# Windowed attention and a gated feed-forward block on one core: score bursts of three head pairs and paired value bursts at fixed places, half 1 reordered, batch 1's products on VectorE

## The chip, the cores and the metric

The kernel runs on one core of a Trainium2 chip. The metric is the device time of one execution in microseconds (us). Every kernel was run beside runs of the kernel before on the same chip. Profiles are of one execution each; their span, from the first to the last instruction, is some 1.8 us less than the device time. The record's verdicts call a difference under 2% the same; where I call a smaller one a gain or a loss, its 95% interval lies on one side of 1.

## The reference

Four batches of 8 heads, 768 tokens, head size 64. A query sees 8 global keys and the last 96 keys, with a bias that grows with distance. The attention output, as 3072 tokens of 512, goes through a gated feed-forward block.

```python
def _attn_ref(q, k, v, n_global, n_local):            # (4, 8, 768, 64) each; 8, 96
    scores = scale * np.matmul(q, k.transpose(0, 1, 3, 2))
    rel = pos[:, None] - pos[None, :]
    keep = (pos[None, :] < n_global) | ((rel >= 0) & (rel < n_local))
    scores = np.where(keep, scores - slope * dist, -1e9)
    a = np.exp(scores - scores.max(-1, keepdims=True))
    return np.matmul(a / (a.sum(-1, keepdims=True) + 1e-9), v)

def _moe_ref(x, w_gate, w_val, w_out):                # 512 -> 1536 -> 512
    g = x @ w_gate
    return (g / (1 + np.exp(-g))) * (x @ w_val) @ w_out
```

## The kernel before

The feed-forward block runs in 8 tiles of 384 tokens; a batch is two tiles ("halves"). A tile has 12 rounds: a gate product, a value product and, interleaved, a quarter of an output product of an earlier tile. A round with all three takes 1.95 us. Of the eight PSUM banks, four (a0 to a3, the "a-banks") go round among the bursts, three among gate and value products, and one holds an output product. The attention of the next half is slipped in between as bursts: transposes of q and k (tile 1 alone; later batches are turned by DMA transposes, "turns" below), scores of a head pair (row-tiled, 64*128), and denominators and numerators of a quad of heads (column-tiled, 128*32).

```python
def scores(self, bk, mul_eng, put_off):        # one head pair, one bank of keys
    sc = banks("sc")                           # two of the a-banks of PSUM
    ...                                        # matmuls, two heads side by side
    if put_off: later.append(exps)             # ScalarE: two exps into `at`
    else:       exps()
    later.append(mask)                         # at *= mask, on VectorE or GpSimd

def values(self, half, bank, mul_eng):         # one quad of heads
    den = bank("den"); self.weigh(half, den, None)
    for side in range(2):
        num = bank("num"); self.weigh(half, num, side)
        nc.scalar.copy(out=src, in_=num[:, 0:TB])
    later.append(lambda: self.invert(den))     # VectorE: transpose, reciprocal
    later.append(spread)                       # VectorE: 1/den; then x = num * 1/den
    ...                                        # on VectorE for batch 0, else on GpSimd

def fetch(b, *hps):                            # turn by DMA, issued from SyncE
    if hps[0] == 0: turn_ends(b)               # kE: the last 48 keys of all pairs
    for hp in hps:  pairs[b, hp].transposes_dma()    # kT, qT of pair hp

def first(b):                                  # tile 1
    return [[tr(b, 0), tr(b, 1)], [sc(b, 0, 0), sc(b, 0, 1)], [tr(b, 2), tr(b, 3)],
            [sc(b, 1, 0), sc(b, 1, 1)], [sc(b, 2, 0), sc(b, 2, 1)], [va(b, 0, 0)],
            [sc(b, 3, 0), sc(b, 3, 1)], [], [va(b, 1, 0)]]
# steps are dealt out evenly among the products; `later` is worked off one item per product
```

Loads go out from GpSimd's queue in program order, so a load can stand behind a product that GpSimd has to make. The fourth early output product stands in round 1 of tile 1.

The softmax here doesn't subtract the row's maximum and nothing guards it: scores larger than these inputs give would overflow.

Of the kernel before, what the change touches and what calls it, by code (L numbers as in the profile page):

```python
# [9 lines left out]
FP32 = mybir.dt.float32  # L10
# [27 lines left out]
def kernel(  # L38
# [117 lines left out]
    def stage_rows(b):  # L156
        qst[b] = sb2.tile([128, NP, J, 2, D], FP16, name="qst", tag="qst")
        kst[b] = sb2.tile([128, NP, J, 2, D], FP16, name="kst", tag="kst")
        kend[b] = sb2.tile([128, H, D], FP16, name="kend", tag="kend", bufs=1)
        nc.gpsimd.memset(kend[b], 0.0)  # L160
        nc.sync.dma_start(out=kend[b][0:NG], in_=kG[:, b])
        for hp in range(NP):
            pair = kG[:, b, 2 * hp:2 * hp + 2, :].rearrange("p h d -> p (h d)")
            nc.sync.dma_start(
                out=kst[b][0:NG, hp].rearrange("p t e d -> p t (e d)"),
                in_=pair.unsqueeze(1).broadcast_to([NG, J, 2 * D]))
# [9 lines left out]
    kG = sb.tile([NG, B, H, D], FP16, name="kG")  # L176

    def load_globals():
        for dst, src in ((kG, k), (vG, v)):
            nc.gpsimd.dma_start(  # L180
                out=dst[:, 1:].rearrange("p b h d -> p (b h) d"),
                in_=src[1:, :, 0:NG, :].rearrange("b h p d -> p (b h) d"))
# [55 lines left out]
    def banks(name, dt=FP32):  # L238
        return [bank(name, dt) for _ in range(2)]

# [15 lines left out]
    class Pair:  # L256
# [97 lines left out]
        def scores(self, bk, mul_eng, put_off):  # L354
            hp = self.hp
            sc = banks("sc")
# [45 lines left out]
    class Quad:  # L402
# [33 lines left out]
        def invert(self, den):  # L436
            dT = sb2.tile([128, TB], FP32, name="dT", tag="dT")
            self.dR = sb2.tile([128, TB // 32], FP32, name="dR", tag="dR")
            nc.vector.transpose(dT, den[:, 0:TB])  # L439
            nc.vector.reciprocal(  # L440
                out=self.dR, in_=dT.rearrange("p (n i) -> p n i", i=32)[:, :, 0])
# [10 lines left out]
        def values(self, half, bank, mul_eng):  # L452
# [3 lines left out]
            for side in range(2):  # L456
                num = bank("num")
                self.weigh(half, num, side)
                src = sb2.tile([128, TB], FP32, name="ns", tag="ns")
                nc.scalar.copy(out=src, in_=num[:, 0:TB])  # L460
                srcs.append(src)
# [25 lines left out]

    hTs = {}
# [3 lines left out]
    def products(t, f, which, c0, c1, dst=None):  # L492
        if f == 0 and which == 0 and c0 == 0:
            hTs[t] = sb2.tile([128, NFF, TB], FP16, name="hT", tag="hT", bufs=3)
        if c0 == 0:
            if dst is None:
                dst = single("gv"[which] + "ps", state["x"][gv.get("n", 0) % len(state["x"])])
                gv["n"] = gv.get("n", 0) + 1
            gv[f, which] = dst
# [141 lines left out]
    def sc(b, hp, bk):  # L641
        on_vector = b < 2 or bk < 2 or hp % 2 == 0
        return lambda: pairs[b, hp].scores(bk, nc.vector if on_vector else nc.gpsimd, bool(later))

    def va(b, g, half):
        return lambda: quads[b, g].values(half, bank, nc.vector if b == 0 else nc.gpsimd)
# [17 lines left out]
    def second(b):  # L664
        return [[sc(b, 0, 2), sc(b, 1, 2)], [sc(b, 2, 2), sc(b, 3, 2)],
                [va(b, 0, 1)], [va(b, 1, 1)]]

# [8 lines left out]
    def first(b):  # L676
        return [[tr(b, 0), tr(b, 1)], [sc(b, 0, 0), sc(b, 0, 1)], [tr(b, 2), tr(b, 3)],
                [sc(b, 1, 0), sc(b, 1, 1)], [sc(b, 2, 0), sc(b, 2, 1)], [va(b, 0, 0)],
                [sc(b, 3, 0), sc(b, 3, 1)], [], [va(b, 1, 0)]]

    def both(b):

        n = b + 1

        return [[sc(b, 0, 2), sc(b, 1, 2)], [sc(b, 2, 2), sc(b, 3, 2), fetch(n, 0, 1)],
                [va(b, 0, 1)], [va(b, 1, 1)],
                [sc(n, 0, 0), sc(n, 0, 1), fetch(n, 2, 3)], [sc(n, 1, 0), sc(n, 1, 1)],
                [va(n, 0, 0)], [sc(n, 2, 0), sc(n, 2, 1)],
                [sc(n, 3, 0), sc(n, 3, 1)], [va(n, 1, 0)]]

    half1 = [[trh(0), trh(1)], [trh(2), trh(3)], [sch(0)], [sch(1)],
             [va(0, 0, 1)], [sch(2)], [sch(3)], [va(0, 1, 1)]]
# [3 lines left out]
    def ff(t, f0, f1, n_out=(0,)):  # L696
# [5 lines left out]
        (ff(1, 0, 12, (0, 1, 1, 1)), first(1), 5.0, 0.2),  # L702
        (ff(2, 0, 12, (1,)) + ff(3, 0, 12, (1,)), both(1), 6.0, 0.4),
        (ff(4, 0, 12, (1,)) + ff(5, 0, 12, (1,)), both(2), 6.0, 0.4),
        (ff(6, 0, 12, (1,)), second(3), 6.0, 0.4),
# [14 lines left out]
    for b, base, rate, v_at in ((2, 19, 2.0, (27, 28, 29, 30, 32, 33, 34)), (3, 43, 1.4, (54, 55, 56, 57, 61, 62, 63))):  # L720
# [12 lines left out]
    outs = [(t, i, part) for t in range(NT - 1) for i in range(3) for part in range(4)]  # L733
    for tiles, steps, tail, owed in stretches:
        groups = []
# [3 lines left out]
        work = sum(g[0] for g in groups)  # L739
        quota = len(steps) / (work - tail)  # L740
        for w, t, f, which in groups:
# [8 lines left out]
            else:  # L750
                gate_or_val(t, f, which, NC if t == 0 and f < 2 else 0)
                for fn in after.pop((t, f, which), []):
                    fn()
            owed += w * quota
            while owed >= 1.0 and steps:
                run_later(len(later))
                for step in steps.pop(0):
                    step()
# [42 lines left out]
```

## Time and profile before

| | before |
|---|---|
| device time, median of 6 runs | 248.66 us (247.84 to 250.19) |
| span of the profile | 247.4 us |
| TensorE busy | 96% |
| VectorE, ScalarE, GpSimd busy | 65%, 53%, 47% |

TensorE streams nearly all the time, so the questions are where it waits and what a burst costs beside its own streaming. The waits of TensorE (who waited for whom: us in total, times, longest) and the granted clock in 40 slices (9 is 90% of full speed or more) of the kernel before:

```profile
PE trs L293 <- DMA q<-in_q_dram: 1.4, 3, 0.6
...
PE gps L502 <- POOL xT L464: 1.1, 2, 0.6
...
PE num L429 <- DMA vS<-in_v_dram: 0.6, 1, 0.6
...
PEclk9999999999999999999999999999999999999999
```

### The profile page before, as it was taken

To read this page: it belongs to the slowest core of one execution; us is meant where nothing else is said; L and a number is where in the kernel's file an instruction comes from. 1 tells how busy PE (TensorE), PEld (TensorE's weight loads), DVE (VectorE), ACT (ScalarE), POOL (GpSimd) and SP (SyncE) were. 2 spreads that over 40 slices of the span, in tenths; PEclk is the share of its full clock that TensorE was granted. 3 is DMA by queue.
4 is the path that set the end of the run, shared out by engine and by line. 5 is a ranking of instruction groups with operands and counts; after the bars stand their busy time and mean duration, and the time that the engine had idled before them with its cause. 6 is when DMAs were issued, how large, how long until landed. Compare 5 with 4: busy or idle time off the path is not lost.

```text
span 247.4 us, 6076 instructions
## 1 busy us (share of the span) xinstructions
PE 238.3 (96%) x2428; PEld 134.8 (54%) x2428; DVE 159.9 (65%) x346; ACT 130.2 (53%) x289; POOL 116.2 (47%) x139
## 2 busy tenths in 40 slices
PE   8898889999998999999999999999999999999994
PEld 5454455555554555555555555555555555555543
DVE  5778656678784767776775576676766666555510
ACT  5736568786753644555734734656635534332321
POOL 8999895344199915407429678603030342200000
PEclk9999999999999999999999999999999999999999
DMA  8999999999279998912919999921001101100122
GB/s 154 164 175 168 186 166 194 202 163 141 69 55 141 137 166 119 146 51 51 85 45 107 82 156 178 176 54 44 30 15 45 42 3 42 43 21 24 42 88 85
DMA packets 86644, 25.10 MB, mean 101 GB/s; under 512 B 72800, under 2 KB 83672, under 8 KB 86616
## 3 DMA queue, kind: packets, MB, share of 16 engines
q0 software_dynamic: 67472, 14.05, 68.0%
q1 hardware_dynamic: 18584, 10.30, 18.1%
q8 instruction: 19, 0.31, 0.6%
q10 hardware_dynamic: 560, 0.36, 0.5%
q14 instruction: 9, 0.07, 0.1%
HBM read 28.67 MB, written 6.29 MB: 141 GB/s over the span
## 4 chain that ended last, share of the span: by engine, by line
PE 74%; DMA 12%; POOL 10%; issue 1%; DVE 0%; ACT 0%; POOLq 0%
PE ops L531 23%; PE vps L502 21%; PE gps L502 21%; DMA qst<-in_q_dram 5%; DMA vS<-in_v_dram 5%; PE sc L365 3%; DMA q<-in_q_dram 3%; PE num L429 3%; PE den L429 2%; POOL vS L170 1%; POOL wv L212 1%; POOL xT L464 1%; POOL k L118 1%; POOL qst L193 1%; PE trs L267 1%
## 5 line engine op out<-in xcount | busy, mean ns | idle before, releaser
L515 DVE SCALAR_TENSOR_TENSOR sl<-th,gps 128x384 f32<-128x384 f32 x94 | 52.0, 553 | 51.9 <-ACT th L513 51.2
L513 ACT ACTIVATE th<-gps 128x384 f32<-128x384 f32 x94 | 46.4, 494 | 65.9 <-PE gps L502 64.2
L502 PE MATMUL gps<-xT,wg 128*128 128x384 f16 x376 | 77.2, 326 | 1.4 <-POOL xT L464 1.1
L502 PE MATMUL vps<-xT,wv 128*128 128x384 f16 x376 | 76.6, 326 | 0.6 <-DVE sl L515 0.6
L531 PE MATMUL ops<-wo,hT 128*128 128x512 f16 x276 | 73.1, 379 | 0.0
L519 DVE TENSOR_TENSOR hT<-vps,sl 128x384 f16<-128x384 f32 x94 | 51.9, 552 | 10.3 <-PE vps L502 3.0
L464 POOL TENSOR_TENSOR xT<-ns,rb 128x384 f16<-128x384 f32 x24 | 23.8, 1014 | 69.2 <-DVE rb L445 69.2
L502 PEld LDWEIGHTS <-wg 128*128 128x128 f16 x384 | 36.3, 98 | 33.4 <-issue 1.7
L502 PEld LDWEIGHTS <-wv 128*128 128x128 f16 x384 | 36.1, 98 | 27.0 <-issue 3.3
L531 PEld LDWEIGHTS <-hT 128*128 128x128 f16 x276 | 26.2, 98 | 23.7 <-issue 0.7
L373 ACT ACTIVATE at<-sc 128x432 f16<-128x432 f32 x72 | 33.2, 536 | 9.6 <-PE sc L365 9.6
L170 POOL DMA_DIRECT2D vS<-in_v_dram x28 | 24.8, 899 | 7.5 <-DMA wo<-in_moe_w_out_dram 3.5
L537 ACT ACTIVATE osb<-ops 128x512 f32<-128x512 f32 x23 | 13.7, 598 | 17.1 <-PE ops L531 17.1
L460 ACT COPY ns<-num 128x384 f32<-128x384 f32 x28 | 12.1, 483 | 9.4 <-PE num L429 8.5
L384 DVE TENSOR_TENSOR at<-at,masks 128x864 f16<-128x864 f16 x20 | 12.1, 607 | 7.0 <-ACT at L373 7.0
L193 POOL DMA_DIRECT2D kst<-in_k_dram x16 | 14.1, 888 | 0.0
L193 POOL DMA_DIRECT2D qst<-in_q_dram x16 | 13.7, 867 | 0.0
L384 POOL TENSOR_TENSOR at<-at,masks 128x864 f16<-128x864 f16 x4 | 7.3, 1821 | 13.3 <-ACT at L373 13.3
L348 ACT ACTIVATE at<-sc 128x432 f16<-128x432 f32 (+2 forms) x32 | 11.6, 447 | 3.0 <-PE sc L340 2.8
L429 PE MATMUL num<-at,vS 128*32 128x216 f16 (+6 forms) x560 | 12.3, 226 | 0.6 <-DMA vS<-in_v_dram 0.6
L429 PEld LDWEIGHTS <-vS 128*32 128x32 f16 x560 | 9.7, 95 | 1.2 <-DMA vS<-in_v_dram 1.0
L439 DVE STREAM_TRANSPOSE dT<-den 128x384 f32<-128x384 f32 x16 | 9.2, 578 | 1.6 <-PE den L429 1.6
(71 smaller groups left out, 175.0 us busy)
## 6 DMA issues: line engine op xcount, KB each, us to landing
out_dram<-osb SPq DMA_DIRECT2D x23, 256.0 KB
vS<-in_v_dram POOLq DMA_DIRECT2D x24, 120.0 KB, 6.2
wg<-in_moe_w_gate_dram POOLq DMA_DIRECT2D x12, 128.0 KB, 5.3
wv<-in_moe_w_val_dram POOLq DMA_DIRECT2D x12, 128.0 KB, 5.3
wo<-in_moe_w_out_dram POOLq DMA_DIRECT2D x4, 384.0 KB, 9.2
qst<-in_q_dram POOLq DMA_DIRECT2D x16, 96.0 KB, 3.6
kst<-in_k_dram POOLq DMA_DIRECT2D x16, 90.0 KB, 3.7
kst<-in_k_dram POOLq DMA_DIRECT2D x2, 384.0 KB, 13.0
```

What stands on the lines that cost most here:

```text
L170: nc.gpsimd.dma_start(out=vSs[b][NG:NG + n, c, :, :], in_=v[b, :, KC * c:KC * c + n, :].rearrange("h p d -> p h d"))
L193: nc.gpsimd.dma_start(out=st[b][p0:p0 + n, h // 2, :, h % 2, :], in_=src[b, h, 0:n * J].rearrange("(t p) d -> p t d", p=n))
L373: nc.scalar.activation(out=at[:, hi, :], in_=sc[hi][:, 0:BANK], func=AF.Exp, scale=scale)
L384: mul_eng.tensor_mul(at, at, m[:, :, o:o + BANK])
L429: nc.tensor.matmul(dst[r, o:o + n], lhsT=ones[:, 0:32] if side is None else vals[:, 4 * g + j, side::2], rhs=pairs[b, 2 * g + j // 2].at[c ...
L464: mul_eng.tensor_mul(self.x_out(half, side), srcs[side], self.rb)
L502: nc.tensor.matmul(gv[f, which][:, 0:TB], lhsT=w[:, c, 128 * f:128 * f + 128], rhs=x_of(t)[:, c, :], start=(c == 0), stop=(c == NC - 1))
L513: nc.scalar.activation(out=th, in_=dst[:, 0:TB], func=AF.Tanh, scale=0.5)
L515: nc.vector.scalar_tensor_tensor(out=sl, in0=th, scalar=1.0, in1=dst[:, 0:TB], op0=AluOp.add, op1=AluOp.mult)
L519: nc.vector.tensor_mul(hTs[t][:, f, :], dst[:, 0:TB], gv["sl"])
L531: nc.tensor.matmul(ops, lhsT=hTs[t][:, f, 128 * i:128 * i + 128], rhs=wo[:, f, :], start=(f == 0), stop=(f == NFF - 1))
L537: nc.scalar.mul(out=osb, in_=ops, mul=0.5)
```

## The change

Its intent is to switch TensorE's tiling less often: three head pairs to a score burst, two quads to a value burst, each at a fixed place behind an output product. Two spare PSUM banks of the gate and value products serve the first pair. Half 1 of batch 0 is reordered. Products of x for batch 1 move from GpSimd to VectorE, those of a paired burst are shared between the two, and the loads of batch 3 are placed earlier. The rest of the diff is room: dT has one buffer in place of two, ns four, and kG goes without batch 0. The core of the diff:

```diff
+    def spare(name):                       # one of the three banks of gate and value
+        tag = state["x"][gv.get("n", 0) % len(state["x"])]
...
+    def both_values(b, half):              # two denominators, inverted at once, then
+        ...                                # four numerators; first quad's x on GpSimd,
+                                           # second quad's on VectorE
     def va(b, g, half):
-        return lambda: quads[b, g].values(half, bank, nc.vector if b == 0 else nc.gpsimd)
+        return lambda: quads[b, g].values(half, bank, nc.vector if b < 2 else nc.gpsimd)
...
-    def first(b):
-        return [[tr(b, 0), tr(b, 1)], [sc(b, 0, 0), sc(b, 0, 1)], [tr(b, 2), tr(b, 3)], ...
+    def first(t, b):                       # (tile, round): behind that round's products
+        return {(t, 1): [tr(b, 0), tr(b, 1)],
+                (t, 3): [sc(b, (0, 0), (0, 1), (1, 0))],
+                (t, 4): [tr(b, 2), tr(b, 3)],
+                (t, 6): [sc(b, (1, 1), (2, 0), (2, 1))],
+                (t, 7): [va(b, 0, 0)],
+                (t, 8): [sc(b, (3, 0), (3, 1))],
+                (t, 9): [va(b, 1, 0)]}
+    def both(t, b):
+        n = b + 1
+        return {(t, 0): [sc(b, (0, 2), (1, 2), (2, 2)), fetch(n, 0, 1)],
+                (t, 4): [sc(b, (3, 2), (0, 0, n), (1, 0, n)), fetch(n, 2, 3)],
+                (t, 8): [vas(b, 1)],
+                (t + 1, 0): [sc(n, (0, 1), (1, 1), (2, 0))],
+                (t + 1, 4): [sc(n, (2, 1), (3, 0), (3, 1))],
+                (t + 1, 8): [vas(n, 0)]}
...
-    half1 = [[trh(0), trh(1)], [trh(2), trh(3)], [sch(0)], [sch(1)],
-             [va(0, 0, 1)], [sch(2)], [sch(3)], [va(0, 1, 1)]]
+    half1 = [[trh(0), trh(1)], [sch(0)], [trh(2), trh(3)], [sch(1)],
+             [sch(2)], [va(0, 0, 1)], [sch(3)], [va(0, 1, 1)]]
...                                         # batch 3's loads of q, k (base) and v (list)
-    (3, 43, 1.4, (54, 55, 56, 57, 61, 62, 63))
+    (3, 35, 1.6, (47, 48, 49, 50, 51, 52, 53))
```

More of the change, by code (lines that the diff above doesn't have):

```diff
@@ L160, in stage_rows @@
         nc.gpsimd.memset(kend[b], 0.0)
-        nc.sync.dma_start(out=kend[b][0:NG], in_=kG[:, b])
+        nc.sync.dma_start(out=kend[b][0:NG], in_=kG[:, b - 1])
         for hp in range(NP):
-            pair = kG[:, b, 2 * hp:2 * hp + 2, :].rearrange("p h d -> p (h d)")
+            pair = kG[:, b - 1, 2 * hp:2 * hp + 2, :].rearrange("p h d -> p (h d)")
             nc.sync.dma_start(
@@ L175 @@
     vG = sb.tile([NG, B, H, D], FP16, name="vG")
-    kG = sb.tile([NG, B, H, D], FP16, name="kG")
+    kG = sb.tile([NG, B - 1, H, D], FP16, name="kG")
     def load_globals():
-        for dst, src in ((kG, k), (vG, v)):
+        for dst, src in ((kG, k), (vG[:, 1:], v)):
             nc.gpsimd.dma_start(
-                out=dst[:, 1:].rearrange("p b h d -> p (b h) d"),
+                out=dst.rearrange("p b h d -> p (b h) d"),
                 in_=src[1:, :, 0:NG, :].rearrange("b h p d -> p (b h) d"))
@@ L239, in banks @@
         return [bank(name, dt) for _ in range(2)]
+    def spare(name):
+        tag = state["x"][gv.get("n", 0) % len(state["x"])]
+        gv["n"] = gv.get("n", 0) + 1
+        return single(name, tag)
     def single(name, tag, dt=FP32):
@@ L352, in scores_half, with scores @@
                 nc.vector.tensor_mul(at, at, masks[:, 2 * hp:2 * hp + 2, WIN:WIN + BANK])
-        def scores(self, bk, mul_eng, put_off):
+        def scores(self, bk, mul_eng, put_off, sc):
             hp = self.hp
-            sc = banks("sc")
             for c in range(NCH):
@@ L436, in invert @@
         def invert(self, den):
-            dT = sb2.tile([128, TB], FP32, name="dT", tag="dT")
+            dT = sb2.tile([128, TB], FP32, name="dT", tag="dT", bufs=1)
             self.dR = sb2.tile([128, TB // 32], FP32, name="dR", tag="dR")
@@ L458, in values @@
                 self.weigh(half, num, side)
-                src = sb2.tile([128, TB], FP32, name="ns", tag="ns")
+                src = sb2.tile([128, TB], FP32, name="ns", tag="ns", bufs=4)
                 nc.scalar.copy(out=src, in_=num[:, 0:TB])
@@ L485, in numerators, with scale_num, spread_first @@
             nc.vector.tensor_mul(self.x_out(0, side), num[:, 0:TB], self.rb)
+    def both_values(b, half):
+        two = [quads[b, g] for g in range(2)]
+        for quad in two:
+            den = spare("den")
+            quad.weigh(half, den, None)
+            quad.invert(den)
+        srcs = {}
+        for g, quad in enumerate(two):
+            for side in range(2):
+                num = bank("num")
+                quad.weigh(half, num, side)
+                src = sb2.tile([128, TB], FP32, name="ns", tag="ns", bufs=4)
+                nc.scalar.copy(out=src, in_=num[:, 0:TB])
+                srcs[g, side] = src
+        def scale_num(eng, g, side):
+            eng.tensor_mul(two[g].x_out(half, side), srcs[g, side], two[g].rb)
+        def spread_first():
+            two[0].spread()
+            for side in range(2):
+                scale_num(nc.gpsimd, 0, side)
+        later.append(spread_first)
+        later.append(two[1].spread)
+        for side in range(2):
+            later.append(lambda side=side: scale_num(nc.vector, 1, side))
     hTs = {}
@@ L496, in products @@
             if dst is None:
-                dst = single("gv"[which] + "ps", state["x"][gv.get("n", 0) % len(state["x"])])
-                gv["n"] = gv.get("n", 0) + 1
+                dst = spare("gv"[which] + "ps")
             gv[f, which] = dst
@@ L637, with sc, step, vas @@
                 products(0, f, which, c0, c1, hb[f][which])
-    def sc(b, hp, bk):
-        on_vector = b < 2 or bk < 2 or hp % 2 == 0
-        return lambda: pairs[b, hp].scores(bk, nc.vector if on_vector else nc.gpsimd, bool(later))
+    def sc(b, *units):
+        def step():
+            for i, (hp, bk, *other) in enumerate(units):
+                pair = pairs[b + 1 if other else b, hp]
+                on_vector = pair.b < 2 or bk < 2 or hp % 2 == 0
+                pair.scores(bk, nc.vector if on_vector else nc.gpsimd, bool(later),
+                            [spare("sc") for _ in range(2)] if len(units) == 3 and i == 0
+                            else banks("sc"))
+        return step
     def va(b, g, half):
-        return lambda: quads[b, g].values(half, bank, nc.vector if b == 0 else nc.gpsimd)
+        return lambda: quads[b, g].values(half, bank, nc.vector if b < 2 else nc.gpsimd)
+    def vas(b, half):
+        return lambda: both_values(b, half)
     def tr(b, hp):
@@ L662, in sch @@
         return step
-    def second(b):
-        return [[sc(b, 0, 2), sc(b, 1, 2)], [sc(b, 2, 2), sc(b, 3, 2)],
-                [va(b, 0, 1)], [va(b, 1, 1)]]
     def fetch(b, *hps):
@@ L674, in fetch, with second @@
         return step
-    def first(b):
-        return [[tr(b, 0), tr(b, 1)], [sc(b, 0, 0), sc(b, 0, 1)], [tr(b, 2), tr(b, 3)],
-                [sc(b, 1, 0), sc(b, 1, 1)], [sc(b, 2, 0), sc(b, 2, 1)], [va(b, 0, 0)],
-                [sc(b, 3, 0), sc(b, 3, 1)], [], [va(b, 1, 0)]]
-    def both(b):
-        n = b + 1
-        return [[sc(b, 0, 2), sc(b, 1, 2)], [sc(b, 2, 2), sc(b, 3, 2), fetch(n, 0, 1)],
-                [va(b, 0, 1)], [va(b, 1, 1)],
-                [sc(n, 0, 0), sc(n, 0, 1), fetch(n, 2, 3)], [sc(n, 1, 0), sc(n, 1, 1)],
-                [va(n, 0, 0)], [sc(n, 2, 0), sc(n, 2, 1)],
-                [sc(n, 3, 0), sc(n, 3, 1)], [va(n, 1, 0)]]
-    half1 = [[trh(0), trh(1)], [trh(2), trh(3)], [sch(0)], [sch(1)],
-             [va(0, 0, 1)], [sch(2)], [sch(3)], [va(0, 1, 1)]]
+    def first(t, b):
[7 more added lines that the diff above has]
+    def both(t, b):
+        n = b + 1
+        return {(t, 0): [sc(b, (0, 2), (1, 2), (2, 2)), fetch(n, 0, 1)],
[4 more added lines that the diff above has]
+                (t + 1, 8): [vas(n, 0)]}
+    def second(t, b):
+        return {(t, 0): [sc(b, (0, 2), (1, 2))], (t, 3): [sc(b, (2, 2), (3, 2))],
+                (t, 7): [vas(b, 1)]}
+    half1 = [[trh(0), trh(1)], [sch(0)], [trh(2), trh(3)], [sch(1)],
+             [sch(2)], [va(0, 0, 1)], [sch(3)], [va(0, 1, 1)]]
     def ff(t, f0, f1, n_out=(0,)):
@@ L701 @@
         (ff(0, 4, 11) + [(0, 11, 3)], half1, 4.7, 0.4),
-        (ff(1, 0, 12, (0, 1, 1, 1)), first(1), 5.0, 0.2),
-        (ff(2, 0, 12, (1,)) + ff(3, 0, 12, (1,)), both(1), 6.0, 0.4),
-        (ff(4, 0, 12, (1,)) + ff(5, 0, 12, (1,)), both(2), 6.0, 0.4),
-        (ff(6, 0, 12, (1,)), second(3), 6.0, 0.4),
+        (ff(1, 0, 12, (0, 1, 1, 1)), first(1, 1), 0, 0),
+        (ff(2, 0, 12, (1,)) + ff(3, 0, 12, (1,)), both(2, 1), 0, 0),
+        (ff(4, 0, 12, (1,)) + ff(5, 0, 12, (1,)), both(4, 2), 0, 0),
+        (ff(6, 0, 12, (1,)), second(6, 3), 0, 0),
         (ff(7, 0, 12, (1,)), [], 0, 0)]
@@ L719 @@
     at_step(1, 1, lambda: [copy_globals(b) for b in range(1, B)])
-    for b, base, rate, v_at in ((2, 19, 2.0, (27, 28, 29, 30, 32, 33, 34)), (3, 43, 1.4, (54, 55, 56, 57, 61, 62, 63))):
+    for b, base, rate, v_at in ((2, 19, 2.0, (27, 28, 29, 30, 31, 32, 33)), (3, 35, 1.6, (47, 48, 49, 50, 51, 52, 53))):
         items = [(base, lambda b=b: stage_rows(b)), (base + 1, lambda b=b: load_ends(b))]
@@ L733, with take @@
     outs = [(t, i, part) for t in range(NT - 1) for i in range(3) for part in range(4)]
+    def take(step_list):
+        run_later(len(later))
+        for step in step_list:
+            step()
     for tiles, steps, tail, owed in stretches:
+        fixed = isinstance(steps, dict)
         groups = []
@@ L738 @@
             groups += [(1.1, t, f, 2)] * n_out
-        work = sum(g[0] for g in groups)
-        quota = len(steps) / (work - tail)
-        for w, t, f, which in groups:
+        quota = 0 if fixed else len(steps) / (sum(g[0] for g in groups) - tail)
+        for i, (w, t, f, which) in enumerate(groups):
             if which == 0:
@@ L753 @@
                     fn()
+            if fixed:
+                if (t, f) in steps and groups[i + 1][1:3] != (t, f):
+                    take(steps.pop((t, f)))
+                continue
             owed += w * quota
             while owed >= 1.0 and steps:
-                run_later(len(later))
-                for step in steps.pop(0):
-                    step()
+                take(steps.pop(0))
                 owed -= 1.0
```

## The prediction

> **What bounds the kernel now.** I read the page first, then the waits, then TensorE's timeline, since the page's busy row hides what matters.
>
> ```profile
> PE 238.3 (96%) x2428; PEld 134.8 (54%) x2428; DVE 159.9 (65%) x346; ACT 130.2 (53%) x289; POOL 116.2 (47%) x139
> ```
>
> TensorE is busy 96% of a 247.4 us span (the run took 249.19 us, the median is 249.27). The change leaves its number of instructions the same, so it can only win or lose gaps between them. The ends of matmuls are modelled, so I count from start to start. Around a score burst (columns: start, duration, engine, line, operation, tiles, shape, count):
>
> ```profile
> 99.17 0.81 PE L531 MATMUL ops<-wo,hT 128*128 128x512 f16 x3
> 99.81 0.81 PE L502 MATMUL gps<-xT,wg 128*128 128x384 f16 x4
> 100.56 0.54 PE L365 MATMUL sc<-qT,kT 64*128 64x216 f16 x8
> 101.04 0.82 PE L502 MATMUL vps<-xT,wv 128*128 128x384 f16 x4
> 101.70 0.81 PE L531 MATMUL ops<-wo,hT 128*128 128x512 f16 x3
> ```
>
> The reader is to see a beat of 0.65 us for a gate, value or output product, broken around the burst: 99.81 to 100.56 is 0.75, so 0.10 is lost on entry. The burst takes 0.48; its 8 matmuls of 216 columns run two at a time, 4 x 0.0925 = 0.37 (at the rate found below), so 0.11 is lost on leaving. One score burst thus costs 0.22 us, with 0.01 in the product after it. A value burst of 16 and 32 matmuls (110.16 to 111.09, after an entry of 0.09) takes 0.93 for 0.78 of streaming: 0.25 us in all.
>
> The one long stall is where tile 2 begins:
>
> ```profile
> 75.28 1.99 POOL L464 TENSOR_TENSOR xT<-ns,rb 128x384 f16<-128x384 f32 x2
> 75.45 0.49 PE L502 MATMUL gps<-xT,wg 128*128 128x384 f16 x2
> ...
> 76.38 0.32 PE L502 MATMUL gps<-xT,wg 128*128 128x384 f16 x1 [0.43 <-POOL xT L464]
> ...
> 77.32 0.32 PE L502 MATMUL gps<-xT,wg 128*128 128x384 f16 x1 [0.62 <-POOL xT L464]
> 77.48 0.81 PE L502 MATMUL vps<-xT,wv 128*128 128x384 f16 x4
> ```
>
> A product that should take 0.65 takes 2.03: **1.38 us** lost to GpSimd, which makes the last two quarters of x between load issues.
>
> Before that, TensorE is paced by loads that no part of the change makes come sooner:
>
> ```profile
> 45.42 0.92 POOL L170 DMA_DIRECT2D vS<-in_v_dram  x1 [2.46 <-DMA wo<-in_moe_w_out_dram]
> ...
> 48.70 0.53 PE L267 MATMUL trs<-ident,qst 128*64 128x128 f16 x12 [0.18 <-DMA qst<-in_q_dram]
> ...
> 49.83 0.82 PE L502 MATMUL vps<-xT,wv 128*128 128x384 f16 x4
> ...
> 50.62 0.81 PE L531 MATMUL ops<-wo,hT 128*128 128x512 f16 x3
> ...
> 50.86 0.90 POOL L170 DMA_DIRECT2D vS<-in_v_dram  x1 [1.01 <-DMA wo<-in_moe_w_out_dram]
> ```
>
> GpSimd is released by the third part of wo just before 45.42 (it landed at 45.14 by the records) and by the fourth just before 50.86 (50.57). The third early output product starts at 45.18, the fourth at 50.62: each 0.04 to 0.05 us after its weights. Both are gated by the load.
>
> **What the Trainium skill says.** "TensorE: Matmul & The Clock Gate", Back-to-back issue gap, gives N/2.4 + 2.5 ns for a warm matmul: 162.5 ns at 384 columns, 0.65 us for four. The trace agrees to 0.01 us. "TensorEngine Tiling (Array Packing)", Key Properties: changing the tiling mode drains TensorE. The trace agrees: the products run as 128*128, scores as 64*128, values as 128*32, and each change costs about 0.1 us. "Perfetto Trace Analysis", Tensor Engine Instruction, says that the profiler's end is an estimate; the trace shows durations of 0.81 in a beat of 0.65, so I use starts. "Trainium Kernel Development and Optimization", Best Practices, says consistent bubbles can mean that PSUM ran out; before, no such wait appears on TensorE, after I expect one (below).
>
> **The change part by part.** I compared the order of the two built programs.
>
> *Fewer bursts.* From tile 1 on there were 32 bursts (2 transposes, 18 scores, 12 values), now 22 (2, 13, 7). Saved: 5 x 0.22 + 5 x 0.25 = 2.35 us, of which one score burst (0.22) lies in tile 1 and 4 x 0.22 + 5 x 0.25 = 2.1 later. That later part is on the path: there TensorE does nothing but stream.
>
> *Batch 1 products on VectorE.* Eight products of 0.548 us (the four of batch 0 on VectorE measure that) go there in place of 1.014 on GpSimd for the quads of tile 1's end; the later quad pairs are shared between the two. VectorE has room (65%). The stall of 1.38 us goes. GpSimd also no longer sits waiting for rb between load issues, so the loads of batch 2 go out earlier.
>
> *Half 1 reordered.* It takes away a wait of 0.6 us of the value burst for v and 0.5 us of the transposes for q, about 1 us. But three output products follow, and the third still waits for wo until 45.18. So this gains nearly nothing: 0.1 us at the start of tile 1.
>
> *Tile 1, fixed places.* Before, the first transposes (48 matmuls, 1.46 us and 0.2 of switching) stood ahead of the fourth output product and filled the wait for its wo. Now the order is g v g v o, then transposes. Tile 1 starts at 45.85, four products end at 48.45, and the output product cannot start before 50.62: TensorE idles 2.1 us. The transposes come after it: 1.66 us lie behind the gate that lay ahead of it. That eats the 0.22 and the 1.38: 76.83 before (the moment when tile 2's first product would have started without its stall) becomes 50.62 + (76.83 - 50.62 - 1.38 + 1.66 - 0.22) = 76.9.
>
> *New waits in tile 1.* A burst of three pairs takes two spare banks and all four a-banks, and the exps of its second and third pair are put off. Two exps take about 0.95:
>
> ```profile
> 58.05 0.54 PE L365 MATMUL sc<-qT,kT 64*128 64x216 f16 x8
> 58.16 0.49 ACT L513 ACTIVATE th<-gps 128x384 f32<-128x384 f32 x1 [1.24 <-PE gps L502]
> ...
> 58.54 1.80 ACT L373 ACTIVATE at<-sc 128x432 f16<-128x432 f32 x4
> ```
>
> (a) The second transposes stand only one gate and one value product behind such a burst. Counting from the burst: exps of pair one 0.40 to 1.35, tanh of the next gate 1.5 to 2.0, exps of the second unit to 2.9, of the third to 3.85. TensorE is there at 0.66 + 1.30 + 0.09 = 2.05 and needs those banks: it waits 0.9, then 0.2 more, 1.1 us. ScalarE and VectorE run late after it and cost about 0.25 in a product. (b) The first value burst needs three of the banks of the units just before: 0.4 us. (c) The second value burst now stands 3 products behind the scores that it reads, not 6. Scores, two exps, tanh, two exps (to 2.8 us after the burst), then VectorE's sl and hT in order before the mask (0.67): done at 3.8. TensorE needs the first half of it at 2.7 and waits about 1.05. Sum of (a) to (c): 2.8 us; tile 2 starts at about 79.7 against 76.83.
>
> *Tiles 2 to 7.* I laid the same durations along one burst of three: the bank of the gate is free 1.94 us after the gate starts, and the burst comes at 2.04, so it fits. Output banks are emptied right before the bursts, not inside them. The paired value bursts fit too. One thing may not: the keys of batch 3 for the first two pairs are turned by DMA only after the burst at tile 4's start, and are needed four rounds (of gate, value and output product, 1.95 us each) later, 9.0 us after that burst began. Five turns go out 1.25 us apart, and the last lands about 3 us after its issue (last pair before: 155.24 to 158.2 in the DMA records): 0.8 + 5.0 + 3.0 = 8.8 us, and v loads run beside it. I put 0.9 us. Batch 2's are earlier by the head start of its loads.
>
> *Sum, in us against before:* tile 2 starts at +2.8; later bursts -2.1; small bubbles where a tile starts (0.07 twice) -0.1; turned keys +0.9: +1.5 at full size. Some of the stalls of tile 1 may overlap more than I counted, so I take +1.0: 249.27 + 1.0 = 250.3.
>
> **The rivals.** *The intent holds:* 2.3 from bursts and 1.4 from the stall, perhaps 1 from half 1, nothing new: 244.6. For it speaks that each term is seen in the trace; against it, that wo's fourth part gates an instruction in program order, so that the 1.4 and the 1 cannot both show. *Loads gate, but the bank and mask waits are hidden:* 249.27 + 0.1 - 2.2 = 247.1. For it: the durations are sure to a tenth only; against it: the programs' order shows these waits on ScalarE and VectorE. *VectorE becomes the bound* in tile 1, where it is already at 80% (9.61 and 9.96 us of 12 in the windows from 48 to 72): 2 us more, 252; I see 1.2 us per value burst added, which fits. *The turned keys come late at both tiles, 2 and 4:* 252 to 253.
>
> **Range and chances.** Between the second rival (247.1) and all stalls at full size with late keys (252.5) lies my range, 247.5 to 252.5. Faster by over 2% needs 244.3, below what the load gate allows: 0.02. Slower by over 2% needs 254.2, twice my sum of stalls: 0.03.
>
> **What would show it.** Right: output product four at about 50.6 with the transposes behind it and TensorE idle for about 2 us before; waits of TensorE on exps in the second transposes, and of a denominator on a mask; tile 2's start without a wait on GpSimd but at 78 to 80; from there to the end 1 to 2 us less than before. Wrong: tile 2 starting before 76.5, which would mean that wo landed earlier; or waits of scores on turned keys over 2 us.

## More of the kernel before

The trace records the clock that TensorE was granted; "half clock" is a granted share of 0.50.

I also use one more measure: the length of a tile, from the start of its first gate product to the start of the next tile's. For the kernel before, tiles 1 to 6 take 29.63, 28.84, 27.17, 27.47, 27.17 and 26.82 us.

## The result

The changed kernel took 256.46 us (median of 6 runs, 254.67 to 258.13) against 248.66 us before. Ratios here are the mean time of one kernel's runs over the mean of the other's runs of the same rounds, so not quite the ratio of the medians. Executions over 1.5% slower than the fastest of the same kernel are left out of the means. The ratio is 1.0303, with a 95% interval of 1.0241 to 1.0365: slower by 3%. I had predicted 250.3, within 247.5 to 252.5.

The profiled execution was the longest of the six (258.13 us, span 256.3). It is not an odd one: a window of half clock of 3.41 us takes 0.007 from the mean granted clock of a span of 256 us (half of 3.41 over 256), and the six runs had 0.980 to 0.993, so by this estimate each had one to three such windows. Its page, busy shares first, then busy tenths and clock in 40 slices of 6.4 us:

```profile
PE 238.9 (93%) x2428; PEld 137.3 (54%) x2428; DVE 167.3 (65%) x360; ACT 129.3 (50%) x289; POOL 102.1 (40%) x125
...
PE   7897999598998999999999949999999999999995
...
PEclk9999999979999999999999979999999999999999
```

TensorE has two holes, the "5" (the slice from 44.9 us) and the "4" (from 147.4 us). The clock falls to 7 in the slice behind the first and in the slice of the second. The waits of TensorE name them:

```profile
PE sc L369 <- DMA qT<-qst: 3.8, 1, 3.8
PE ops L562 <- DMA wo<-in_moe_w_out_dram: 3.3, 2, 2.3
...
PE den L433 <- DVE at L385: 1.1, 1, 1.1
PE trs L272 <- ACT at L377: 0.8, 1, 0.8
```

All four are waits that the prediction named; a wait of scores on turned keys of over 2 us was its own sign of being wrong. Tile lengths say how much each stretch lost or won (us, counted from the traces):

| kernel | tile 1 starts | tile 1 | 2 | 3 | 4 | 5 | 6 |
|---|---|---|---|---|---|---|---|
| before | 45.82 | 29.63 | 28.84 | 27.17 | 27.47 | 27.17 | 26.82 |
| changed | 46.56 | 35.81 | 26.97 | 26.75 | 32.38 | 26.75 | 26.60 |
| difference | +0.74 | +6.18 | -1.87 | -0.42 | +4.91 | -0.42 | -0.22 |

These add up to the whole 8.9 us between the spans. Where no new wait stands (tiles 2, 3, 5, 6), the change wins what it was made for: in tile 2 the stall on GpSimd (1.38) and 0.49 for the bursts. Tiles 1 and 4 lose it several times over.

**Tile 1, round 1**, of the changed kernel in time:

```profile
48.55 0.81 PE L533 MATMUL vps<-xT,wv 128*128 128x384 f16 x4
...
51.67 1.44 PE L562 MATMUL ops<-wo,hT 128*128 128x512 f16 x3 [2.31 <-DMA wo<-in_moe_w_out_dram]
...
53.04 0.85 PE L272 MATMUL trs<-ident,kst 128*64 128x128 f16 x12
```

The output product waits 2.3 us for the last part of wo, which landed at 51.63, and then takes 1.37 us from start to start, where with the switch to transposes 0.74 is usual (e10 below). The clock records grant half speed from 51.69 to 55.10. The transposes take 2.43 us in place of 1.46. So the half clock costs 0.63 + 0.97 = 1.6 us on top of the wait.

**Tile 1, round 9.** What VectorE did before the second denominator:

```profile
74.51 1.01 DVE L468 TENSOR_TENSOR xT<-ns,rb 128x384 f16<-128x384 f32 x2
...
75.44 0.60 DVE L388 TENSOR_TENSOR at<-at,masks 128x864 f16<-128x864 f16 x1
...
77.08 0.67 DVE L385 TENSOR_TENSOR at<-at,masks 128x432 f16<-128x432 f16 x2
77.51 0.48 PE L433 MATMUL den<-at,ones 128*32 128x144 f16 x6 [1.05 <-DVE at L385]
```

The denominator loses 1.90 us in all, against the 1.05 of the prediction. In the trace VectorE takes its work in program order, and the two products of x that the change gave it (1.01 us) stand ahead of the masks.

**Tile 4.** The turned keys of batch 3 (SyncE's queue), the v loads on GpSimd, and TensorE:

```profile
138.95 1.22 SPq L203 DMA_TRANSPOSE kE<-kend  x1
...
142.87 3.42 POOL L170 DMA_DIRECT2D vS<-in_v_dram  x4
...
144.29 1.75 SPq L401 DMA_TRANSPOSE qT<-qst  x1
...
146.89 0.19 PE L369 MATMUL sc<-qT,kE 64*128 64x48 f16 x2
...
151.08 0.55 PE L369 MATMUL sc<-qT,kT 64*128 64x216 f16 x4 [3.82 <-DMA qT<-qst]
151.56 1.46 PE L533 MATMUL gps<-xT,wg 128*128 128x384 f16 x4
...
152.81 1.44 PE L533 MATMUL vps<-xT,wv 128*128 128x384 f16 x4
```

Five turns are issued from 138.95 on; the last, issued at 144.29, lands only at 150.94 by the records, 6.65 us later. TensorE waits 3.8 us for it (from start to start the burst takes 4.84 us, where it takes 0.66 in e9), and the two products behind it take 1.25 and 1.28 us at half clock (150.67 to 154.09), 1.2 us more. Beside the turns run four v loads.

The same lines show a slip that has nothing to do with time. kE is overwritten with batch 3's keys at 138.95, and at 146.89 the last pair of batch 2 reads it. Those scores use the wrong keys for 48 positions of two heads. The comparison with the reference passed all the same; how much the output moves was not measured. Three of the experiments below also put that right.

### The profile page after: what moved, and what is told of

It reads as the page before. It is cut to its first block, busy times and chain, and to the rows that moved or that the text cites. A ratio compares the mean times of both kernels' runs of the same rounds, so it can differ in the third digit from the quotient of the medians.

```text
span 256.3 us, 6051 instructions
## 1 busy us (share of the span) xinstructions
PE 238.9 (93%) x2428; PEld 137.3 (54%) x2428; DVE 167.3 (65%) x360; ACT 129.3 (50%) x289; POOL 102.1 (40%) x125
## 4 chain that ended last, share of the span: by engine, by line
PE 70%; DMA 13%; POOL 8%; DVE 3%; SPq 2%; issue 1%; ACT 1%; DVEq 0%; POOLq 0%
PE ops L562 21%; PE gps L533 20%; PE vps L533 19%; DMA wo<-in_moe_w_out_dram 5%; PE sc L369 3%; DMA q<-in_q_dram 3%; DMA vS<-in_v_dram 3%; DMA qT<-qst 3%; PE num L433 2%; POOL wv L212 2%; POOL vS L170 2%; PE trs L272 2%; SPq L401 1%; PE den L433 1%; POOL wg L212 1%
## 5 line engine op out<-in xcount | busy, mean ns | idle before, releaser
L562 PE MATMUL ops<-wo,hT 128*128 128x512 f16 x276 | 73.9, 382 | 3.3 <-DMA wo<-in_moe_w_out_dram 3.3
L533 PEld LDWEIGHTS <-wg 128*128 128x128 f16 x384 | 35.6, 98 | 32.3 <-issue 2.1
L533 PEld LDWEIGHTS <-wv 128*128 128x128 f16 x384 | 37.3, 98 | 26.4 <-issue 2.3
L508 POOL TENSOR_TENSOR xT<-ns,rb 128x384 f16<-128x384 f32 x10 | 9.8, 996 | 81.8 <-DVE rb L449 61.6
L562 PEld LDWEIGHTS <-hT 128*128 128x128 f16 x276 | 27.1, 98 | 28.0 <-issue 4.8
L369 PE MATMUL sc<-qT,kT 64*128 64x216 f16 (+2 forms) x152 | 9.3, 250 | 3.8 <-DMA qT<-qst 3.8
L504 ACT COPY ns<-num 128x384 f32<-128x384 f32 x20 | 8.1, 493 | 7.9 <-PE num L433 7.9
L433 PE MATMUL num<-at,vS 128*32 128x216 f16 (+6 forms) x560 | 11.2, 226 | 0.0
L385 DVE TENSOR_TENSOR at<-at,masks 128x432 f16<-128x432 f16 x24 | 8.1, 377 | 4.4 <-ACT at L377 4.4
```

Source lines behind the costliest of these rows:

```text
L369: nc.tensor.matmul(sc[hi][:, col:col + n], lhsT=keys, rhs=self.qT[r, q0:q0 + n], start=True, stop=True)
L433: nc.tensor.matmul(dst[r, o:o + n], lhsT=ones[:, 0:32] if side is None else vals[:, 4 * g + j, side::2], rhs=pairs[b, 2 * g + j // 2].at[c ...
L533: nc.tensor.matmul(gv[f, which][:, 0:TB], lhsT=w[:, c, 128 * f:128 * f + 128], rhs=x_of(t)[:, c, :], start=(c == 0), stop=(c == NC - 1))
L562: nc.tensor.matmul(ops, lhsT=hTs[t][:, f, 128 * i:128 * i + 128], rhs=wo[:, f, :], start=(f == 0), stop=(f == NFF - 1))
```

## The experiments

My theory: the losses are four separate ones. (1) The last turn in tile 4 is late because v loads crowd it and because it is fifth in its queue. (2) The fourth output product waits for wo, and the transposes behind it are thereby late. (3) Long waits bring a window of half clock. (4) Two waits in tile 1 come from put-off exps and from VectorE's order. Rivals were that turns are slow by themselves, that the order in tile 1 makes no difference because the load paces all, that the clock drops for another reason, and that a paired burst costs somewhere else.

### e1: the turn of the last keys later

```diff
     def fetch(b, *hps):
-            if hps[0] == 0:
-                turn_ends(b)
             for hp in hps:
                 pairs[b, hp].transposes_dma()
+            if hps[0] == 2:
+                turn_ends(b)
```

> The changed kernel with one edit: the turn of the last keys (kE) of the next batch is issued after the turns of its pairs 2 and 3, not ahead of those of pairs 0 and 1. The four turns that tile 4's second burst waits for then start 1.33 us earlier and are done before the v loads crowd in. My theory (the stall is a queue position plus crowding): the wait of scores on qT at about 147 us falls from 3.8 us to under 0.5, the clock window at half speed beside it (3.41 us) goes, the span falls by 4 to 5.5 us. Rival (a turn of q and k simply takes over 6 us from issue to landing, whatever runs beside it): the wait falls by 1.3 us to about 2.5.

Measured: 252.70 us (ratio to before 1.0136, 1.0086 to 1.0186).

```profile
138.33 3.40 POOL L170 DMA_DIRECT2D vS<-in_v_dram  x4
138.59 2.81 SPq L401 DMA_TRANSPOSE qT<-qst  x1
...
145.91 0.27 PE L369 MATMUL sc<-qT,kT 64*128 64x216 f16 x2 [3.19 <-DMA qT<-qst]
```

The wait on qT fell only to 3.2 us. This missed my number, and sides with the rival's more than with mine. The first three turns went out earlier, but the last was issued at 138.59, beside v loads that began at 138.33. Its issue took 2.81 us where 1.21 is usual, and TensorE got its scores at 145.91, 7.3 us after that issue. So a place nearer the front is not enough. Tile 4 took 32.02 us, hardly less than 32.38. Most of the gain in this trace is therefore not this edit's: here wo landed at 48.68, tile 1 began at 44.05, and it took 33.79 us without a half-clock window. The other three runs have no trace, and the fastest of them (251.46 us) had a granted clock of 1.000, so no half-clock window at all. What the edit gave on average stays open. How early wo lands differs from run to run (48.58 to 51.63 in the traces here).

### e2: batch 3's v loads early

```diff
-    (3, 35, 1.6, (47, 48, 49, 50, 51, 52, 53))
+    (3, 35, 1.6, (44, 44, 44, 44, 44, 44, 44))
```

> The changed kernel with one edit: all seven v loads of batch 3 are placed before GpSimd's x products of tile 3, so they are done before tile 4 begins, where four of them were held behind a mask product on GpSimd and ran beside the turned keys. Crowding theory: the last turn lands about 3 us after its issue at 144.3 (it took 6.65), the wait of 3.8 us falls to under 0.5, the span by 4 to 5.5 us. Rival (turns are slow by themselves): the landing stays over 6 us after the issue and the wait stays over 3 us.

Measured: 252.08 us (ratio 1.0118, 1.0068 to 1.0168). Tile 4 took 27.84 us in place of 32.38.

```profile
143.06 1.94 SPq L401 DMA_TRANSPOSE qT<-qst  x1
...
146.73 0.36 PE L369 MATMUL sc<-qT,kT 64*128 64x216 f16 x4 [0.69 <-DMA qT<-qst]
```

With the same five turns in the same order, the last landed at 146.59, 3.5 us after its issue, and the wait was 0.7 us in place of 3.8. It came a little over the 0.5 that I expected. Tile 1, left alone, took the same 35.81 us, again with a wait for wo (2.4 us) and half clock behind it (51.00 to 54.41). The rival, slow by themselves, falls: what made the turns slow were the four v loads beside them. The Trainium skill, "DMA: Bandwidth & Descriptors", Issuing engines are not separate DMA queues, says that transfers issued from different engines run on the same 16 DMA engines and interleave; these two runs agree, 6.65 us with v loads beside the turn and 3.5 without. The loads ran there because they stood behind a mask product on GpSimd, which waits for exps of the burst.

### e3: tile 1's first transposes ahead of the output product

```diff
-                if (t, f) in steps and groups[i + 1][1:3] != (t, f):
+                if (t, f) in steps and (which == 1 if (t, f) == (1, 1)
+                                        else groups[i + 1][1:3] != (t, f)):
```

> The changed kernel with one edit: in tile 1 the first transposes stand ahead of the fourth output product again, not behind it. Theory (that output product waits for the last part of wo, and the transposes behind it add their 1.66 us plus what the half clock costs): the idle time before the output product falls from 2.3 us to under 1, no half-clock window follows, the span falls by 2 to 3.5 us. Rival (the load paces everything, the order of the two makes no difference): the span falls by under 0.5 us.

Measured: 254.37 us, 253.53 for the three fast runs (ratio 1.0179, 1.0105 to 1.0252, unclear at 2%); by the ratios some 3 us less than the changed kernel.

```profile
49.57 0.50 PE L272 MATMUL trs<-ident,qst 128*64 128x128 f16 x12
50.65 0.81 PE L562 MATMUL ops<-wo,hT 128*128 128x512 f16 x3 [0.57 <-DMA wo<-in_moe_w_out_dram]
```

The transposes fill the wait again, 0.6 us of it is left, no half-clock window follows, and tile 1 takes 32.48 us. The theory holds, the rival falls. In this trace the key wait in tile 4 happened to be larger (5.2 us, tile 4 33.65), so its span shows less than the 3.3 us that tile 1 won.

### e4: half 1 in the old order

```diff
-    half1 = [[trh(0), trh(1)], [sch(0)], [trh(2), trh(3)], [sch(1)],
-             [sch(2)], [va(0, 0, 1)], [sch(3)], [va(0, 1, 1)]]
+    half1 = [[trh(0), trh(1)], [trh(2), trh(3)], [sch(0)], [sch(1)],
+             [va(0, 0, 1)], [sch(2)], [sch(3)], [va(0, 1, 1)]]
```

> The changed kernel with the order of half 1 of the kernel before. Theory: the reordered half 1 is ready about 1 us earlier but the third early output product waits for wo anyway, so the time stays within 0.5 us of the changed kernel (ratio to before 1.025 to 1.035), and tile 1 starts at the same moment. Rival (half 1's gain reaches the end): 1 us slower.

Measured: 257.06 us (ratio 1.0322, 1.0273 to 1.0370), within 0.6 us of the changed kernel and not resolved from it. The time is as expected, the reason only half so. In this trace wo's third part landed at 42.72, and the third output product still came at 45.05, so TensorE's own work set that start, not the load. In e1, where that part landed at 42.95, the new order began tile 1 at 44.05, against 45.69 here, with the same start of tile 0's products (15.25 and 15.30). So the reordered half 1 does gain some 1.6 us there when the load is early. The fourth output product takes it back: its weights landed at 48.68 and 49.05, and TensorE waited 1.8 us in e1 and 0.5 us here.

### e5: the second transposes one round later

```diff
-                (t, 4): [tr(b, 2), tr(b, 3)],
+                (t, 5): [tr(b, 2), tr(b, 3)],
```

> The changed kernel with one edit: in tile 1 the second transposes stand one round later (behind round 5, not round 4). Bank theory (they need the four banks whose exps were put off behind the three-pair burst): the wait of 0.8 us of the transposes on ScalarE's exps, and the 0.2 us inside the transposes, go; nothing takes their place, as the next score burst is still a round away; tile 1 is 1.0 us shorter than in a run with the same load wait. Rival (ScalarE is simply full there and the wait moves to the next product or burst): tile 1 stays as long, another wait of 0.8 us appears within two rounds.

254.76 us. The wait of the transposes on exps is gone. The next score burst now loses 0.44 us in place of 0.11, though. Tile 1 took 33.20 us, against 33.79 in e1, which had a like wait for wo (1.9 and 1.8 us) and no half-clock window either. So 0.6 us were won of the 1.0 that the wait had cost (0.85 ahead of the transposes, 0.18 in them). The bank theory is right for the wait itself, and about a third of it moved on, as the rival said.

### e6: the products back on GpSimd

```diff
-        return lambda: quads[b, g].values(half, bank, nc.vector if b < 2 else nc.gpsimd)
+        return lambda: quads[b, g].values(half, bank, nc.vector if b < 1 else nc.gpsimd)
```

> The changed kernel with batch 1's half-0 products of x back on GpSimd. Queue theory (the products and the spread of the first quad stand ahead of the masks in VectorE's order, which is what made the second denominator wait 1.9 us in place of the 1.05 that I predicted): the loss in that denominator falls to 0.9 to 1.2 us, and a wait on GpSimd's x of 0.5 to 1.4 us comes back where tile 2 begins. Rival (the mask is late for another reason): the denominator still loses 1.9 us.

One look, with a surprise: the single time was 264.19 us. The denominator lost 1.61 us, between my number and the rival's, and where tile 2 begins the first product lost only 0.2 us (78.95 to 79.79 for 0.65).

```profile
71.16 2.32 POOL L468 TENSOR_TENSOR xT<-ns,rb 128x384 f16<-128x384 f32 x2 [10.68 <-DVE rb L449]
71.37 1.24 DVE L388 TENSOR_TENSOR at<-at,masks 128x864 f16<-128x864 f16 x1
...
PE sc L369 <- DMA qT<-qst: 9.8, 3, 5.0
```

The queue theory is thus shown for 0.3 us only. The first two lines show why the mask was not much earlier: beside GpSimd's product it took 1.24 us on VectorE, and 0.60 in the changed kernel. The third, from the waits of TensorE, shows the surprise: now the turned keys come late in tile 2 as well, and tile 2 took 34.42 us in place of 26.97. GpSimd sat idle 10.7 us before the product while batch 2's loads stood behind it, and those loads then ran beside batch 2's turns. So in this one trace the move to VectorE is worth some 7.5 us in tile 2 (two windows of half clock are part of it), far more than the stall that I saw it remove. In the kernel before, the first two pairs' turns were issued from 80.55 to 85.04 and used from 100.56 on, some 16 us later, so such a delay would have been hidden there.

### e8: the kernel before with the products on VectorE alone

```diff
-        return lambda: quads[b, g].values(half, bank, nc.vector if b == 0 else nc.gpsimd)
+        return lambda: quads[b, g].values(half, bank, nc.vector if b < 2 else nc.gpsimd)
```

> The kernel before with one part of the change alone: batch 1's products of x on VectorE in all quads. Theory: the stall of 1.38 us where tile 2 begins goes, tile 1 is no longer than 29.9 us, ratio to before 0.992 to 0.997. Rival (VectorE's queue grows and masks come late): tile 1 grows by as much as the stall was, ratio 0.998 to 1.004.

Measured: 248.33 us (ratio 0.9960, 0.9922 to 0.9999). Tile 2 took 27.47 us in place of 28.84: the 1.37 us of the stall are gone. Tile 1 grew to 30.15 from 29.63. Of that growth, 0.2 us is wo, which landed later after the tile's start, and 0.27 a value product that waits for VectorE. Theory and rival both have a part: the net gain is 0.85 us.

### e9: three mends

The edits of e1, e2 and e3 together.

> The changed kernel with three edits together: the turn of the last keys later, the v loads of batch 3 early, the first transposes of tile 1 ahead of the fourth output product. Everything else of the change stays, the burst places of tile 1 too. Theory (the losses are separate and add): tile 1 about 32.5 us (the waits of the second transposes on exps and of the denominator on a mask remain, 1 and 1.9 us), tile 4 27.0 to 27.3, no half-clock window after the first 10 us, span about 247, ratio to before 0.992 to 1.004, so 2 to 3 us over the version with tile 1 as before. Rival (mending one brings out another): tile 4 over 28 us or tile 1 over 33.5.

Measured: 247.62 us (ratio 0.9958, 0.9919 to 0.9998). Tile 1 took 32.65 us and tile 4 26.98, the clock was whole after the first 6 us, span 246.3. All as expected: the losses are separate and add up, and mending them brought out no other. The two waits that it keeps, of the second transposes and of the denominator, are in its list with 0.8 and 1.1 us.

### e10: matmuls in the wait for wo

```diff
             if which == 2:
+                if (t, f) == (1, 1):
+                    idle = single("warm", f"a{state['n'] % 4}")
+                    for _ in range(16):
+                        nc.tensor.matmul(idle[:, 0:256], lhsT=ones[:, 0:128],
+                                         rhs=ones[:, 0:256], start=True, stop=True)
                 out_part(*outs.pop(0))
```

> The changed kernel with 16 matmuls of 256 columns on ones (1.75 us, thrown away) ahead of the fourth output product, so that TensorE works while it would wait for wo; the product itself can start no earlier. Theory (the half-clock window of 3.41 us beside that wait comes from TensorE's idleness): the wait shrinks from 2.3 us to about 0.6, no half-clock window follows it, the output product takes 0.65 and not 1.37 us and the transposes behind it 1.6 and not 2.4, tile 1 is 34.0 to 34.3 us against 35.81. Rival (the clock drops for another reason): the window is still there and the product behind it still takes over 1.2 us.

Measured, in the trace:

```profile
49.04 1.91 PE L801 MATMUL warm<-ones 128*128 128x256 f16 x16
51.50 0.81 PE L562 MATMUL ops<-wo,hT 128*128 128x512 f16 x3 [0.55 <-DMA wo<-in_moe_w_out_dram]
52.24 0.53 PE L272 MATMUL trs<-ident,kst 128*64 128x128 f16 x12
```

The output product starts right after its weights landed (51.46) and takes 0.74 us with the switch to the transposes, which take 1.46; no half-clock window stands there; tile 1 took 34.20 us, 1.6 less than in the changed kernel. This is the theory to the tenth: here the half clock came from TensorE's idleness. The time of the whole, 257.03 us (ratio 1.0320), is no better, as this trace waits 5.7 us for the turned keys, which the edit leaves alone, with half clock after it from 148.16 to 154.99.

### e7: the change where it gains, tile 1 as before

The edits of e1 and e2, and tile 1 with the places of the kernel before (shortened):

```diff
-    def first(t, b): return {(t, 1): ..., (t, 9): ...}
+    def first(b): return [[tr(b, 0), tr(b, 1)], [sc(b, (0, 0), (0, 1))], [tr(b, 2), tr(b, 3)],
+                          [sc(b, (1, 0), (1, 1))], [sc(b, (2, 0), (2, 1))], [va(b, 0, 0)],
+                          [sc(b, (3, 0), (3, 1))], [], [va(b, 1, 0)]]
```

> The change kept where it gains and taken back where it loses: bursts of three and paired values in tiles 2 to 6, products on VectorE, reordered half 1, but tile 1 with the places of the kernel before, the turn of the last keys behind those of pairs 2 and 3, and the v loads of batch 3 early. Theory (each lost piece is one of these): tile 1 about 30 us (29.6 before, and no stall on GpSimd after it), tiles 2 to 6 26.97, 26.75, 27.0, 26.75, 26.60, no half-clock window, span about 244.3, time 245.5 to 247, ratio to before 0.985 to 0.993. Rival (paired bursts cost more than they save somewhere that tile lengths don't show, or the products on VectorE make tile 1 longer): ratio at or over 1.0.

Measured: 246.00 us (median of 6, 245.33 to 247.04), ratio 0.9859 with 0.9820 to 0.9899: faster than both kernels, by 1.4% than the one before (with the interval clear of 1). Tiles 1 to 6: 29.39, 26.98, 26.75, 27.23, 26.75, 26.60. Its page:

```profile
PE 237.6 (97%) x2428; PEld 136.6 (56%) x2428; DVE 165.9 (68%) x360; ACT 129.1 (53%) x289; POOL 102.1 (42%) x125
...
PEclk9999999999999999999999999999999999999999
```

The clock is whole from the first record on (13 us). So the bursts of three and the paired values cost nothing hidden, and the rival falls.

| kernel | us (median) | ratio to before | tile 1 | tile 4 |
|---|---|---|---|---|
| changed | 256.46 | 1.0303 | 35.81 | 32.38 |
| e1, turn later | 252.70 | 1.0136 | 33.79 | 32.02 |
| e2, v early | 252.08 | 1.0118 | 35.81 | 27.84 |
| e3, transposes first | 254.37 | 1.0179 | 32.48 | 33.65 |
| e9, all three | 247.62 | 0.9958 | 32.65 | 26.98 |
| e7, tile 1 as before | 246.00 | 0.9859 | 29.39 | 27.23 |

## Why the prediction was wrong

**Right:** the price of a burst. Leaving out the stall of 1.38, tiles 2 to 6 were to win 2.1 us for bursts and 0.1 for small bubbles. With tile 4 as in e9 they took 0.49 + 0.42 + 0.49 + 0.42 + 0.22 = 2.04 us less. The stall on GpSimd went, as e8 shows alone. The output product waited for wo, with the transposes behind it. Wait (a) came where it was said to come and lost 0.85 us ahead of the transposes and 0.18 in them, as 1.1 had it. (c) came too, but larger; of (b) there was 0.07 us in place of 0.4. The rival that the intent holds fell in tile 1 to the gate of wo, as argued, and in tile 4 to the turned keys.

**Wrong, first step: the turned keys**, "I put 0.9 us". It cost 4.2 us in the burst (4.84 less the 0.66 of e9) and 1.2 at half clock behind it. The sum had 0.8 + 5.0 + 3.0 = 8.8 us to the last landing, counted from the burst's start. The first two terms were right (kE 0.81 after the burst began, the last issue 6.15 after it, for which I had 5.8). The third was taken from a turn of the kernel before (155.24 to 158.2) with v packets beside it at first only: by the packet records none ran from 156.0 to 157.5. In the changed kernel, where they ran from 145.9 to 150.9 beside the turn, it was 6.65 us. I had named those loads; the 0.9 us of wait allowed about 1.1 for them (8.8 to the landing, 9.0 to the need). e2 shows that they are the cause: without them the term is 3.5 us. That tile 4 of e1's trace gained only 0.36 us says the same: here the crowd counted, not the place in the queue.

**Wrong, second step: nothing stood in the sum for the clock.** I took a wait at its own length. Two waits brought 3.41 us of half clock each, which cost 1.6 us in tile 1 and 1.2 in tile 4. e10 shows it for the first, by filling the wait and changing nothing else.

**Wrong, third: term (c) was 1.05 and measured 1.90.** I had written that VectorE's products fit beside its other work. On average they do; in its order they stood ahead of the mask that TensorE was waiting for. That this order made the whole 0.85 is argued from the trace and not shown: e6 took the products away and won 0.3 back. It does show that GpSimd is no better place for them.

**And the last step:** "Some of the stalls of tile 1 may overlap more than I counted, so I take +1.0." That hedge was right for what it named: (b) lost 0.3 less than I said, and the 0.25 in a product behind (a) did not come. It was outweighed. Tile 1 ran 35.81 us, 2.0 over the 33.85 of my sum (79.7 - 45.85): 1.6 is clock, 0.85 is (c), 0.3 is wo landing later after the tile's start than before, less 0.6 for those two and 0.2 of smaller terms. In all, of the 7.4 us between the +1.5 of my sum and the +8.9 of the spans, 4.5 lie in tile 4, 2.0 in tile 1 and 0.7 in a later start of tile 1, as wo's third part landed at 45.88 in place of 45.14 (it varies from run to run, 42.72 to 45.88 in the traces here).

Two readings were loose without harm to the sum. Four products, not eight, go to VectorE at tile 1's end. And 76.83 is the start that counts the stall in (77.48 less 0.65); without its stall tile 2 starts at 75.45.

The fourth rival of the prediction, keys late at both tiles, was nearest in size, yet it happened at tile 4 alone; by e6's one trace, batch 1's products on VectorE kept it from tile 2.

**Still open:** why the issue of the last turn in e1 took 2.81 us, and why wo's last part lands up to 3 us earlier or later from run to run, which may be why the time of the changed kernel spreads more than that of the kernel before (254.67 to 258.13 against 247.84 to 250.19).

## What to carry to other kernels

Before moving a burst on a full engine, list what in program order stands behind each load and what was filling the wait for it; an instruction that waits in order turns a hidden transfer into a visible one. Give a transfer that gates the next burst free DMA engines, not only an early place: bring the bulk loads in before it. Count a wait on TensorE of the length seen here (2.3 us and more) at its length plus the half-speed window that can follow it, and fill or avoid it.

## What the Trainium skill lacked or had wrong

- "TensorE: Matmul & The Clock Gate", Why this matters for your kernels, advises no idle gaps over some 3 us, and the table under What's actually happening has the clock fall after an idle window of about 3.4 us. Here a wait of 2.3 us was enough where it lay within one window: idle from 49.36 to 51.67, half clock from 51.69, exactly 3.41 us long. A wait of 1.9 us (e5) and one of 2.4 us that lay over the edge of two windows (e6) brought none. The free-running window of 3.4 us under the same heading agrees: within every trace the clock's changes lie on a grid of 3.41 us. The share of a window that must be idle is what the page lacks, and idle time alone does not settle it: near the start of e3 and of e8 a window with 1.6 us of it (from 4.3 us on) was followed by half clock.
- "DMA: Bandwidth & Descriptors" says that queues share the 16 engines, but not what a load in small packets does to a turn beside it. A turn of 128x768 elements of 2 bytes landed 3.5 us after its issue with no load beside it (e2), and 6.65 us with four v loads in packets of 128 bytes beside it (8.0 in e3).
- "TensorEngine Tiling (Array Packing)", Key Properties, says that a change of mode drains TensorE but gives no figure. Here each change costs about 0.1 us, a score burst 0.22 us in all.
- "SBUF — State Buffer", Who interferes with whom, has it that a VectorE instruction with two inputs in SBUF contends with one of GpSimd that reads SBUF, but no figure for a mask beside a product: 1.24 us in place of 0.60 in e6, where the product began first. A mask of the kernel before that began while GpSimd's products ran (68.11) took its usual 0.61; there the product that began 0.1 us after it took 1.37 in place of 1.0.
